# Key loads moved to the SP queue and spread over the batch, GpSimd work reordered behind the split of u, and a new deal of the value matmuls in groups that lend a PSUM bank

## The chip, the core and the metric

The kernel runs on one core of a Trainium2 chip. The metric is the device time of one execution in microseconds (us). The core has five engines with a queue of instructions each, worked off in order: TensorE (PE in the profile; its weight loads are PEld), VectorE (DVE), ScalarE (ACT), GpSimd (POOL) and SyncE (SP). SP only issues DMAs here; ACT issues some too. All DMAs are carried by the same 16 DMA engines.

## What is computed

An attention over pooled keys, then a feed-forward layer with a SoLU activation and a layer norm:

```python
kv_pool = kv.reshape(B, H // 4, 4, W // 4, 4, C).mean(axis=(2, 4))
k = v = kv_pool.reshape(B, -1, C) @ w_sr            # 4 batches, 768 keys of 128
s = (q @ k.transpose(0, 2, 1)) / sqrt(C)            # 12288 queries a batch
x = softmax(s) @ v
h = x @ w_in                                        # 128 -> 1024
solu = h * softmax(h)
ln = (solu - mean) / sqrt(var + 1e-6) * g_ln
out = ln @ w_out                                    # 1024 -> 128
```

Inputs are float32 and float64; the kernel works with float16 high and low halves, so most products are three matmuls (high by high, high by low, low by high).

## The kernel before

The queries are cut into 384 tiles of 128 (`NT`), 96 to a batch (`TPB`), four tiles to a group (`GT`). The main loop runs over slots. In one slot every stage of the pipeline does its step for another tile: the scores of tile slot+1 (`scores_pe`), their softmax and its float16 split (`scores_exp`, `scores_split`, which ends in a DMA transpose `pT` on SP), a quarter of the value matmuls of a group (`values`, 18 matmuls of 512 columns to a group), the hidden layer of tile slot-9 (`hidden_pe`), its maximum, exponential, product u, variance (`hidden_max`, `hidden_exp`, `hidden_u`, `hidden_var`) and u's float16 split on POOL (`hidden_split`, two instructions, followed by the DMA transpose `uT` on SP in `hidden_turn`), and the output layer of tile slot-13 (`final_pe`, 24 matmuls of 128 columns). From slot 9 on the order of the instructions on each engine is the order in which the code is written (`tc.manual_schedule`). I name slots by their remainder: 4n+1 is a slot with one more than a multiple of 4.

Once in four slots, on POOL: `q_low` (the low half of the next queries, slot 4n+2), the two small instructions of `final_scale` (tiles `f`, slot 4n+3) after an ACT instruction that they wait for, and `values_norm` (tiles `zz`, slot 4n+1). In slot 4n+1 DVE also does `values_split` (`xl`), `values_recip` (`rz`) and `final_out` (`ob`). On SP, a load of queries (`qf`, 256 KB) stands ahead of the pT of slot 4n+3, a store of results after the uT of slot 4n+1.

While a batch is worked on, the keys and values of the next are prepared by a table, `PLAN`: rows of slot in the batch, half (384 keys each) and functions. Each of 16 summands of the pooling is loaded in two halves of 192 KB by `kv_load` on the ACT queue, one half every second slot from slot 4 to slot 64, and added by `kv_add` on POOL three slots later. When a half has its sum, `kv_k_pe` multiplies it by w_sr, and a chain of small steps on ACT, POOL and DVE follows; half 0 does this from slot 41, half 1 from slot 69. The matmuls of this chain (`kv_k_pe`, `kv_norm_pe`, `kv_v_pe`, the slots in `WITH_PE`: 41, 69, 77, 81, 85, 89) borrow the one PSUM bank in which `values` accumulates (`ps_x`, one buffer), so a group whose values would start in such a slot deals its 18 matmuls 0, 6, 6, 6 over four slots instead of 4, 5, 5, 4. This deal is used in all four batches, though the last one prepares no keys.

PSUM also sets the rhythm of PE: scores and hidden tiles share three buffers (`ps_r`), so `scores_pe` of a slot waits until DVE has done `hidden_u`, and `hidden_pe` until DVE has done `scores_split`.

Of the kernel before, what the change touches and what calls it, by code (L numbers as in the profile page):

```python
# [11 lines left out]
F32 = mybir.dt.float32  # L12
# [27 lines left out]
LAV = 2  # L40
# [4 lines left out]
FSC = 12  # L45
# [7 lines left out]
def kernel(  # L53
# [68 lines left out]
    state = {}  # L122
# [18 lines left out]
    def half_of(name, b, half):  # L141
        return state[name, b][:, half * 384 : half * 384 + 384]
# [31 lines left out]
        )  # L174
        nc.scalar.copy(half_of("kT", 0, half), pk)

    def kv_load(b, part):

        half, pos = divmod(part, RR)
        if pos % 2 == 0:  # L180
            state["kv", b, half, pos // 2] = dmt.tile(
                [P, 2, 384], F32, tag="kvc", name=f"kv_{b}_{part}", bufs=9
            )
        r, two = divmod(pos, 2)
        k0 = two * NK + half * 384
        nc.scalar.dma_start(
            state["kv", b, half, r][:, two, :], kv[b - 1, r, :, k0 : k0 + 384]
        )

    def kv_add(b, part):  # L190

        half, pos = divmod(part, RR)
        t = state["kv", b, half, pos // 2]
        if pos == 1:
            if half == 0:
                state["ka", b] = bat.tile([P, NK], F32, tag="ka", name=f"ka_{b}", bufs=1)
            state["ka", b, half] = half_of("ka", b, half)
            x = state["kv", b, half, 0][:, 0, :]
        else:
            x = state["ka", b, half]  # L200
        nc.gpsimd.tensor_tensor(state["ka", b, half], x, t[:, pos % 2, :], op=ALU.add)

    def kv_psum(b, name):
        pool, tag = (ps_x, "x") if b else (ps_o, "o")
# [119 lines left out]
    def kv_plan(b):  # L324


        plan = {}
        for slot, half, *fs in PLAN:
            plan.setdefault(slot, []).append([partial(f, b, half) for f in fs])
        return plan  # L330


    QL = 1
# [18 lines left out]
    def q_low(g):  # L352
        if g >= NG:
            return
        qf = state["qf", g // QL][:, (g % QL) * 512 : (g % QL + 1) * 512]
        qh, ql = state["q", g]
        nc.gpsimd.tensor_tensor(ql, qf, qh.bitcast(F32), op=ALU.subtract)
# [45 lines left out]
        )  # L403


    def values(g, qtr, part):
        share = {0: [0, 0, 18, 0], 1: [0, 6, 6, 6]}.get(g, [4, 5, 5, 4])
        first = GT * g + GT - 1 + LAV
        if g > 1 and {first % TPB, first % TPB + TPB} & WITH_PE:
            share = [0, 6, 6, 6]  # L410
        s0 = sum(share[:qtr])
        s1 = s0 + share[qtr]
        if s0 == s1:
            return
        cut = s0 + (s0 > 0)
        s0, s1 = ((s0, cut), (cut, s1))[part]
        b = g * GT // TPB
        if s0 == 0 and s1:
            state["xa", g] = ps_x.tile([P, 512], F32, tag="x", name=f"xa_{g}")
        if s0 == s1:  # L420
            return
        xa, pT = state["xa", g], state["pT", g]
        vh, vl = state["vh", b], state["vl", b]
        seq = [(a, c, v) for c in range(NKC) for (a, v) in ((0, vh), (1, vh), (0, vl))]
        for n in range(s0, s1):
            a, c, v = seq[n]
# [149 lines left out]
    def final_scale(g):  # L576

        b = g * GT // TPB
        f = grp.tile([P, GT], F32, tag="f", name=f"f_{g}")
        f2 = grp.tile([P, GT], F32, tag="f2", name=f"f2_{g}")  # L580
        bb = state["bb", b]
        nc.scalar.activation(
            f2, state.pop(("z2", g)), AF.Square, scale=bb[:, 1:2], bias=bb[:, 2:3]
        )
        nc.gpsimd.tensor_tensor(f, f2, state.pop(("v3", g)), op=ALU.add)  # L585
        nc.gpsimd.tensor_tensor(f2, f, mhalf[:, :GT], op=ALU.pow)  # L586
        state["f", g] = f2

    def final_out(g):
        po, f = state.pop(("po", g)), state.pop(("f", g))  # L590
        ob = dmt.tile([P, GT, P], F32, tag="ob", name=f"ob_{g}")
        nc.vector.scalar_tensor_tensor(  # L592
            ob,
            po.rearrange("p (j c) -> p j c", j=GT),
            swi,
            f.unsqueeze(2).to_broadcast([P, GT, P]),
            op0=ALU.mult,
            op1=ALU.mult,
        )
        nc.sync.dma_start(  # L600
            out[g * 512 : (g + 1) * 512, :].rearrange("(j p) c -> p j c", p=P), ob
        )
# [121 lines left out]
    def kv_norms(half):  # L724
# [17 lines left out]

    PLAN = [(4 + 2 * r - 2 * (r // RR), r, kv_load) for r in range(2 * RR)]
    PLAN += [(7 + 2 * r - 2 * (r // RR), r, kv_add) for r in range(2 * RR) if r % RR]
    PLAN += [
        (41, 0, kv_k_pe, kv_k_out), (69, 1, kv_k_pe, kv_k_out),
        (45, 0, kv_ks), (71, 1, kv_ks),
        (48, 0, kv_kh), (72, 1, kv_kh),  # L750
        (52, 0, kv_kl), (74, 1, kv_kl),
        (56, 0, kv_sq), (75, 1, kv_sq),
        (77, 0, kv_scale_v), (78, 1, kv_scale_v), (79, 2, kv_scale_v),
        (79, 0, kv_vs), (81, 1, kv_vs),
        (77, 0, kv_norm_pe, kv_norm_out), (80, 0, kv_norm_max),
        (81, 1, kv_norm_pe, kv_norm_out), (84, 1, kv_norm_max),
        (85, 0, kv_v_pe, kv_norm_out), (87, 0, kv_v_high), (88, 0, kv_v_low),
# [2 lines left out]
    ]  # L760
    WITH_PE = {slot for slot, _, *fs in PLAN if len(fs) > 1}


    def at(t, fn, *args):
        if 0 <= t < NT:
            fn(t, *args)

    def at_last(t, fn, *args):

        if 0 <= t < NT and t % GT == GT - 1:  # L770
            fn(t // GT, *args)

    FRONT = (kv_norm_max, kv_scale_v, kv_bound)
    plan = {}
    by_hand = ExitStack()
    scores_pe(0)
    for slot in range(NT + LO + 2):
# [4 lines left out]
        i = slot - LH  # L782
        av, qtr = divmod(slot - LAV - GT + 1, GT)
        tb, ti = divmod(slot, TPB)
        if ti == 4 and tb + 1 < B:
            for k, v in kv_plan(tb + 1).items():
                plan.setdefault(slot + k - 4, []).extend(v)
        if ti == 12 and tb + 1 < B:
            kv_alloc(tb + 1)
        qs = GT if slot < 3 * GT else 3 * GT + QSP  # L790
# [7 lines left out]
        if 0 <= av < NG:  # L798
            values(av, qtr, 0)
        at(slot + 1, scores_pe)  # L800
        at_last(slot - NORM, values_norm)
        at_last(slot - FSC, final_scale)
        if slot < NT and 0 < qs < slot and (slot - 1 - qs) % GT == 0:
            q_low(slot // GT + 1)
        at(i - 1, hidden_split)
        at(i - 1, hidden_var)
        at(i, hidden_max)
        at(i, hidden_exp)
# [2 lines left out]
        for st in todo:  # L811
            if len(st) > 1:
                st[0]()
        if 0 <= av < NG:
            values(av, qtr, 1)
        for st in todo:
            for f in st[1:]:
# [3 lines left out]
        at_last(slot - NORM, values_recip_u)  # L821
        at(i + 1, hidden_pe)
        at(slot - LO, final_pe)
        at(i - 1, hidden_turn)
        at_last(slot - LO - 1, final_out)
        at_last(slot - XSP, values_out)
# [41 lines left out]
```

## Time and profile before

| what | value |
|---|---|
| median of 3 runs | 1917.81 us (1906.03 to 1918.63) |
| the profiled execution, its own time | 1920.48 us |
| its span (first to last instruction) | 1918.7 us |
| mean granted TensorE clock | 0.993 |
| PE, DVE, ACT, POOL busy | 97%, 93%, 92%, 85% |
| DMA, mean over the span | 226 GB/s |

Busy shares are unions of the instructions' spans on an engine; matmuls are pipelined, so consecutive ones overlap in the records, and a PE that is shown busy throughout streams without a hole. A row of the trace gives the start in us from the span's begin, the duration, the engine, the line in the kernel, and in square brackets the idle time of the engine ahead of it with what ended it. "SPq" is an instruction of SP's queue. Stretches below are named by their window in us.

### The profile page before, as it was taken

To read this page: it belongs to the slowest core of one execution; us is meant where nothing else is said; L and a number is where in the kernel's file an instruction comes from. 1 tells how busy PE (TensorE), PEld (TensorE's weight loads), DVE (VectorE), ACT (ScalarE), POOL (GpSimd) and SP (SyncE) were. 2 spreads that over 40 slices of the span, in tenths; PEclk is the share of its full clock that TensorE was granted. 3 is DMA by queue.
4 is the path that set the end of the run, shared out by engine and by line. 5 is a ranking of instruction groups with operands and counts; after the bars stand their busy time and mean duration, and the time that the engine had idled before them with its cause. 6 is when DMAs were issued, how large, how long until landed. Compare 5 with 4: busy or idle time off the path is not lost. (4 is left out here: it accounts for less than half of the span.)

```text
span 1918.7 us, 43085 instructions
## 1 busy us (share of the span) xinstructions
PE 1855.9 (97%) x15678; PEld 1306.6 (68%) x15678; DVE 1793.5 (93%) x2700; ACT 1760.2 (92%) x3143; POOL 1624.6 (85%) x1392
## 2 busy tenths in 40 slices
PE   7899999999999999999999999999999999999997
PEld 4576666766777666767776666666777776777665
DVE  7999989999999998999999999989999999999985
ACT  4899989999999998999999999989999999999986
POOL 4699989888899998988889989978888888888776
PEclk8999999999999999999999999999999999999999
DMA  6999999999999999999999999999999999999996
GB/s 233 178 244 238 243 228 237 234 221 216 234 240 249 236 229 233 233 237 213 223 229 239 240 229 248 232 223 214 214 225 226 218 230 228 222 223 225 222 200 139
DMA packets 1484308, 432.86 MB, mean 226 GB/s; under 512 B 1405888, under 2 KB 1471552, under 8 KB 1483840
## 3 DMA queue, kind: packets, MB, share of 16 engines
q1 hardware_dynamic: 1469840, 410.10, 108.0%
q10 hardware_dynamic: 14256, 20.00, 4.2%
q8 instruction: 124, 2.03, 0.5%
q14 instruction: 88, 0.72, 0.1%
HBM read 52.50 MB, written 25.17 MB: 40 GB/s over the span
## 5 line engine op out<-in xcount | busy, mean ns | idle before, releaser
L536 POOL TENSOR_TENSOR uhl<-u,uhl 128x1024 f16<-128x1024 f32 x384 | 819.2, 2133 | 38.5 <-ACT uhl L533 7.0
L568 PEld LDWEIGHTS <-uT 128*128 128x128 f16 x9216 | 547.5, 98 | 112.2 <-DMA uT<-uhl 28.4
L568 PE MATMUL o<-wch,uT 128*128 128x128 f16 x6144 | 580.3, 220 | 15.7 <-DMA uT<-uhl 15.7
L568 PE MATMUL o<-wcl,uT 128*128 128x128 f16 x3072 | 537.0, 220 | 0.0
L518 DVE SCALAR_TENSOR_TENSOR u<-h,rz,e 128x1024 f32<-128x1024 f32 x384 | 491.0, 1279 | 30.0 <-ACT e L504 12.6
L488 DVE TENSOR_SCALAR_CACHE_REDUCE junkd<-h,rz 128x1024 bf16<-128x1024 f32 x384 | 491.3, 1279 | 14.5 <-PE h L480 13.2
L504 ACT ACTIVATE e<-h,nm,rz 128x1024 f32<-128x1024 f32 x384 | 458.4, 1194 | 8.0 <-DVE junkd L488 8.0
L549 ACT ACTIVATE junk<-u,su 128x1024 bf16<-128x1024 f32 x384 | 437.7, 1140 | 2.8 <-DVE u L518 2.8
L535 POOL TENSOR_SCALAR uhl<-u 128x1024 f16<-128x1024 f32 x378 | 394.7, 1044 | 29.1 <-DVE u L518 19.3
L387 DVE TENSOR_REDUCE nm<-s 128x1 f32<-128x768 f32 x384 | 365.3, 951 | 50.1 <-PE s L371 44.5
L427 PE MATMUL xa<-pT,vh 128*128 128x512 f16 x1152 | 377.0, 382 | 14.1 <-issue 3.6
L388 ACT ACTIVATE s<-s,nm 128x768 f32<-128x768 f32 x384 | 335.2, 873 | 56.2 <-DVE nm L387 55.3
L398 DVE SCALAR_TENSOR_TENSOR phl<-s,phl 128x768 f16<-128x768 f32 x384 | 366.0, 953 | 5.8 <-ACT phl L390 5.8
L390 ACT ACTIVATE phl<-s 128x768 f16<-128x768 f32 x384 | 311.0, 810 | 12.0
L480 PEld LDWEIGHTS <-xh 128*128 128x128 f16 x1536 | 143.8, 98 | 200.0 <-issue 22.4
L371 PE MATMUL s<-kh,qh 128*128 128x384 f32 x768 | 256.0, 414 | 8.4 <-DVE u L518 3.9
L480 PE MATMUL h<-w_in_h,xh 128*128 128x512 f16 x768 | 229.6, 381 | 10.6 <-DVE rz L462 5.8
L480 PE MATMUL h<-w_in_h,xl 128*128 128x512 f16 x768 | 230.3, 382 | 0.0
L480 PE MATMUL h<-w_in_l,xh 128*128 128x512 f16 x768 | 230.0, 381 | 0.0
L427 PE MATMUL xa<-pT,vl 128*128 128x512 f16 x576 | 219.4, 381 | 0.0
L371 PE MATMUL s<-kh,ql 128*128 128x384 f32 x768 | 197.8, 339 | 0.0
L371 PE MATMUL s<-kl,qh 128*128 128x384 f32 x768 | 195.7, 336 | 0.0
(130 smaller groups left out, 1845.9 us busy)
## 6 DMA issues: line engine op xcount, KB each, us to landing
qf<-in_q_dram SPq DMA_DIRECT2D x96, 256.0 KB, 3.4
out_dram<-ob SPq DMA_DIRECT2D x96, 256.0 KB, 2.9
kv<-in_kv_dram ACTq DMA_DIRECT2D x96, 192.0 KB, 4.0
kv<-in_kv_dram SPq DMA_DIRECT2D x16, 384.0 KB, 8.1
pT<-phl SPq DMA_TRANSPOSE x384, 4.1
uT<-uhl SPq DMA_TRANSPOSE x384, 4.5
raw_in<-in_moe_w_in_dram ACTq DMA_DIRECT2D x1, 1024.0 KB, 6.4
raw_out<-in_moe_w_out_dram SPq DMA_DIRECT2D x1, 1024.0 KB, 7.6
```

The source lines that it names most:

```text
L371: nc.tensor.matmul(s[:, half, :384], lh[:, ts], rh[:, half * 384 : (half + 1) * 384], start=n == 0, stop=n == 2,)
L387: nc.vector.tensor_reduce(nm, s, axis=AX.XY, op=ALU.max, negate=True)
L398: nc.vector.scalar_tensor_tensor(phl[:, 1], state.pop(("s", t)), SC, phl[:, 0], op0=ALU.mult, op1=ALU.subtract)
L427: nc.tensor.matmul(xa, v[:, c, :], pT[:, :, a * NKC + c, :], start=n == 0, stop=n == len(seq) - 1)
L480: nc.tensor.matmul(h[:, hs], lh[:, ts], rh[:, hs], start=n == 0, stop=n == 2)
L488: nc.vector.tensor_scalar(junk, state["h", t], state["rz", g][1][:, j : j + 1], None, op0=ALU.mult, op1=ALU.min, accum_out=nm,)
L504: nc.scalar.activation(e, state["h", t], AF.Exp, bias=nm, scale=state["rz", g][0][:, js], accum_out=state["z2", g][:, js],)
L518: nc.vector.scalar_tensor_tensor(u, state.pop(("h", t)), state["rz", g][2][:, j : j + 1], state.pop(("e", t)), op0=ALU.mult, op1=ALU.mult, ...
L535: nc.gpsimd.tensor_scalar(uhl[:, 0, :], u, 1.0, 1.0, op0=ALU.mult, op1=ALU.mult)
L536: nc.gpsimd.tensor_tensor(uhl[:, 1, :], u, uhl[:, 0, :], op=ALU.subtract)
L549: nc.scalar.activation(junk, u, AF.Square, scale=-float(DFF), bias=su, accum_out=state["v3", g][:, j : j + 1],)
L568: nc.tensor.matmul(po[:, ts], uT[:, a * NFC + c, :], w[:, c, :], start=c == 0 and n == 0, stop=c == NFC - 1 and n == 2,)
```

## The change

1. **Loads.** `kv_load` now loads both halves of a summand at once (384 KB, rows of 3072 B instead of 1536 B) and is issued by SP, at the end of its slot. For batch 1 one load comes every 4 slots from slot 4 to slot 64; for batches 2 and 3 one every 6 slots, from 30 slots before the preceding batch begins (slot 66 of the batch before that) to slot 60 of the preceding batch.
2. **Adds.** The 30 adds of a batch stay, on POOL; the first half's comes 4 slots after its load, the second's 6 slots after. All stand in even slots now; they stood in odd ones.
3. **Key chain.** Both halves go through the chain in slots 69 to 92; half 0 no longer starts in slot 41, half 1 starts its product in slot 73. So the groups that lend their bank are those of slots 69, 73, 77, 81, 85, 89.
4. **Deal of values.** Such a group deals 3, 5, 5, 5, and the first 3 stand at the slot's end, behind `final_pe`. Only batches that prepare keys for another do this; the last batch keeps 4, 5, 5, 4.
5. **POOL order.** The two POOL instructions of `final_scale` become `final_root`, and these and `q_low` are called after `hidden_split`; they stood before it.

```diff
-    def kv_load(b, part):
-        half, pos = divmod(part, RR)
...
-        nc.scalar.dma_start(
-            state["kv", b, half, r][:, two, :], kv[b - 1, r, :, k0 : k0 + 384]
-        )
+    def kv_load(b, pos):
+        t = dmt.tile([P, 2, 384], F32, tag="kvc", name=f"kv_{b}_{pos}", bufs=9)
         r, two = divmod(pos, 2)
+        nc.sync.dma_start(
+            t, kv[b - 1, r, :, two * NK : (two + 1) * NK].rearrange("p (h k) -> p h k", h=2)
+        )
...
+        first, step = (4, 4) if b == 1 else (-30, 6)
+        for pos in range(RR):
+            slot = first + step * pos
+            yield slot, [partial(kv_load, b, pos)]
+            if pos:
+                yield slot + 4, [partial(kv_add, b, 0, pos)]
+                yield slot + 6, [partial(kv_add, b, 1, pos)]
         for slot, half, *fs in PLAN:
+            yield slot, [partial(f, b, half) for f in fs]
...
+    def with_keys(g):
+        b, ti = divmod(GT * g + GT - 1 + LAV, TPB)
+        return g > 1 and b + 1 < B and ti in WITH_PE
...
-        first = GT * g + GT - 1 + LAV
-        if g > 1 and {first % TPB, first % TPB + TPB} & WITH_PE:
-            share = [0, 6, 6, 6]
+        if with_keys(g):
+            share = [3, 5, 5, 5]
...
-        (41, 0, kv_k_pe, kv_k_out), (69, 1, kv_k_pe, kv_k_out),
+        (69, 0, kv_k_pe, kv_k_out), (73, 1, kv_k_pe, kv_k_out),
...
+        at(i - 1, hidden_split)
+        at_last(slot - FSC, final_root)
         if slot < NT and 0 < qs < slot and (slot - 1 - qs) % GT == 0:
             q_low(slot // GT + 1)
-        at(i - 1, hidden_split)
...
-        if 0 <= av < NG:
+        late = 0 <= av < NG and qtr == 0 and with_keys(av)
+        if 0 <= av < NG and not late:
             values(av, qtr, 1)
...
         at(slot - LO, final_pe)
+        if late:
+            values(av, qtr, 1)
```

SP after the change, in the early part of batch 0; `kv` are the loads that stood on ACT's queue, the other names are the transposes, the store (`out`) and the queries (`qf`):

```order
L397 DMA_TRANSPOSE pT_1801<-phl_1775 128x12x128
L542 DMA_TRANSPOSE uT_1835<-uhl_1788 128x16x128
L181 DMA kv_6_1841<-in_kv_dram 128x768
L397 DMA_TRANSPOSE pT_1801<-phl_1846 128x12x128
L542 DMA_TRANSPOSE uT_1916<-uhl_1863 128x16x128
L604 DMA out_dram<-ob_1918 128x4x128
L397 DMA_TRANSPOSE pT_1801<-phl_1927 128x12x128
L542 DMA_TRANSPOSE uT_1988<-uhl_1940 128x16x128
L336 DMA qf_2000<-in_q_dram 128x512
```

A load now stands in the same queue between one slot's uT and the next slot's pT; there was nothing between these two before, and the loads stood on ACT between two exponentials.

POOL over four slots of batch 0, before:

```order
L585 TENSOR_TENSOR f_2605<-f_6_2606,v_6_2183 128x4
L586 TENSOR_TENSOR f_6_2606<-f_2605,mhalf 128x4
L535 TENSOR_SCALAR uhl_2610<-u_2592 128x1024
L536 TENSOR_TENSOR uhl_2610<-u_2592,uhl_2610 128x1024
L201 TENSOR_TENSOR ka_536<-kv_16_2292 128x384
```

and after:

```order
L536 TENSOR_SCALAR uhl_2596<-u_2580 128x1024
L537 TENSOR_TENSOR uhl_2596<-u_2580,uhl_2596 128x1024
L590 TENSOR_TENSOR f_2593<-f_6_2594,v_6_2175 128x4
L591 TENSOR_TENSOR f_6_2594<-f_2593,mhalf 128x4
L536 TENSOR_SCALAR uhl_2664<-u_2653 128x1024
```

The two `f` instructions moved from ahead of a slot's `uhl` pair to behind it; `ql` moved in the same way.

PE in slot 77, the first norm matmul of the key chain (`pn`), after the change, up to the next slot's scores (`s`); `xa` are the values:

```order
L231 MATMUL pn_0_5388<-ksq_619,ones_87 128x384
...
L569 MATMUL o_5404<-wch,uT_5281 128x128
L428 LDWEIGHTS vh_113
L428 MATMUL xa_5429<-pT_5017,vh_113 128x512
...
L428 MATMUL xa_5429<-pT_5017,vl_114 128x512
L428 LDWEIGHTS vh_113
L428 MATMUL xa_5429<-pT_5017,vh_113 128x512
L367 MATMUL s_5453<-kh_105,qh_5140 128x384 x2
```

Four matmuls of values (three of this slot, one of the next) now stand between the output layer's last matmul and the next scores; before, the scores followed the output layer directly.

## Rows read from the trace of the kernel before

**Rows 1.** The page: its head, and part 2's data rate in 40 slices.
```profile
span 1918.7 us, 43085 instructions
GB/s 233 178 244 238 243 228 237 234 221 216 234 240 249 236 229 233 233 237 213 223 229 239 240 229 248 232 223 214 214 225 226 218 230 228 222 223 225 222 200 139
```

**Rows 2.** Windows: from:to, length, busy PE PEld DVE ACT POOL, PEclk, DMA, GB/s.
```profile
1420.00:1600.00 180.00, 180.00 (x1569) 128.14 (x1568) 175.41 (x260) 172.74 (x310) 150.00 (x125) 1.00 1.13 227
712.00:722.00 10.00, 8.04 (x66) 5.37 (x64) 7.68 (x14) 8.06 (x16) 9.56 (x9) 0.83 1.25 239
1255.00:1270.00 15.00, 11.75 (x80) 7.70 (x79) 9.42 (x15) 9.09 (x17) 10.21 (x9) 0.77 1.23 201
```

**Rows 3.** Tile xh, one instruction a group: count, min/median/max ns, first to last start.
```profile
L434 ACT ACTIVATE xh<-xa,sv x9: 687/687/687, 1434.0 to 1583.5; 128x512 f16<-128x512 f32 x9
L434 ACT ACTIVATE xh<-xa,sv x13: 687/687/687, 114.9 to 347.7; 128x512 f16<-128x512 f32 x13
L434 ACT ACTIVATE xh<-xa,sv x11: 687/687/687, 614.4 to 810.3; 128x512 f16<-128x512 f32 x11
L434 ACT ACTIVATE xh<-xa,sv x13: 687/687/687, 1039.8 to 1279.4; 128x512 f16<-128x512 f32 x13
L434 ACT ACTIVATE xh<-xa,sv x7: 687/687/687, 347.7 to 464.9; 128x512 f16<-128x512 f32 x7
L434 ACT ACTIVATE xh<-xa,sv x23: 687/687/687, 1434.0 to 1850.0; 128x512 f16<-128x512 f32 x23
```

**Rows 4.** Waits: engine and line, releaser: us in total, times, longest.
```profile
PEld L568 <- DMA uT<-uhl: 28.4, 33, 3.3
PE o L568 <- DMA uT<-uhl: 15.7, 17, 3.2
```

**Rows 5.** Tile uT: issue to landing, first in 1420:1740, then in 100:350.
```profile
DMA to landing us min/median/max: 3.7/4.0/6.3
DMA to landing us min/median/max: 3.8/4.9/7.6
```

**Rows 6.** Timeline of DVE and SP in 243:262.
```profile
246.38 0.95 DVE L398 SCALAR_TENSOR_TENSOR phl<-s,phl 128x768 f16<-128x768 f32 x1
254.75 1.42 SPq L401 DMA_TRANSPOSE pT<-phl  x1
```

**Rows 7.** Tile pT, SP's issues in 150:317.4 and in 336:372.
```profile
L401 SPq DMA_TRANSPOSE pT<-phl x35: 1279/1465/4191, 150.1 to 317.4; - x35
L401 SPq DMA_TRANSPOSE pT<-phl x9: 1279/1433/1782, 336.6 to 371.5; - x9
```

**Rows 8.** The page, part 6: issues, KB each, median us to landing.
```profile
kv<-in_kv_dram ACTq DMA_DIRECT2D x96, 192.0 KB, 4.0
kv<-in_kv_dram SPq DMA_DIRECT2D x16, 384.0 KB, 8.1
```

**Rows 9.** Waits of POOL for ACT.
```profile
POOL f L585 <- ACT f L582: 129.9, 92, 6.2
POOL ql L357 <- ACT qh L349: 34.0, 39, 8.3
```

**Rows 10.** Timeline of POOL and PE in batch 3, slots 4n+2 and 4n+3.
```profile
1627.42 1.27 POOL L357 TENSOR_TENSOR ql<-qf,qh 128x512 fp32r<-128x512 f32 x1 [1.07 <-ACT qh L349]
1628.67 1.05 POOL L535 TENSOR_SCALAR uhl<-u 128x1024 f16<-128x1024 f32 x1
1629.80 2.13 POOL L536 TENSOR_TENSOR uhl<-u,uhl 128x1024 f16<-128x1024 f32 x1
1634.64 0.51 PE L371 MATMUL s<-kh,ql 128*128 128x384 f32 x2
```

**Rows 11.** Timeline of PE and ACT in batch 0, slots 85 (429 to 432) and 78 (393).
```profile
393.39 0.62 PE L371 MATMUL s<-kh,qh 128*128 128x384 f32 x2 [0.15 <-DVE u L518]
...
429.62 0.59 PE L480 MATMUL h<-w_in_h,xh 128*128 128x512 f16 x2 [0.29 <-DVE rz L462]
429.93 0.47 ACT L245 COPY vf<-pv 128x384 f32<-128x384 f32 x1
432.19 0.22 PE L568 MATMUL o<-wch,uT 128*128 128x128 f16 x1
```

More of the change, by code (lines that the diff above doesn't have):

```diff
@@ L175, in kv_first_k, with kv_add @@
         nc.scalar.copy(half_of("kT", 0, half), pk)
-    def kv_load(b, part):
-        half, pos = divmod(part, RR)
-        if pos % 2 == 0:
-            state["kv", b, half, pos // 2] = dmt.tile(
-                [P, 2, 384], F32, tag="kvc", name=f"kv_{b}_{part}", bufs=9
-            )
+    def kv_load(b, pos):
+        t = dmt.tile([P, 2, 384], F32, tag="kvc", name=f"kv_{b}_{pos}", bufs=9)
         r, two = divmod(pos, 2)
-        k0 = two * NK + half * 384
-        nc.scalar.dma_start(
-            state["kv", b, half, r][:, two, :], kv[b - 1, r, :, k0 : k0 + 384]
-        )
[L190 to L201, printed above, removed]
+        nc.sync.dma_start(
+            t, kv[b - 1, r, :, two * NK : (two + 1) * NK].rearrange("p (h k) -> p h k", h=2)
+        )
+        state["kv", b, pos] = t
+    def kv_add(b, half, pos):
+        if pos == 1 and half == 0:
+            state["ka", b] = bat.tile([P, NK], F32, tag="ka", name=f"ka_{b}", bufs=1)
+        ka = half_of("ka", b, half)
+        x = state["kv", b, 0][:, half, :] if pos == 1 else ka
+        nc.gpsimd.tensor_tensor(ka, x, state["kv", b, pos][:, half, :], op=ALU.add)
     def kv_psum(b, name):
@@ L324, in kv_plan @@
     def kv_plan(b):
-        plan = {}
+        first, step = (4, 4) if b == 1 else (-30, 6)
[5 more added lines that the diff above has]
+                yield slot + 6, [partial(kv_add, b, 1, pos)]
         for slot, half, *fs in PLAN:
-            plan.setdefault(slot, []).append([partial(f, b, half) for f in fs])
-        return plan
+            yield slot, [partial(f, b, half) for f in fs]
     QL = 1
@@ L584, in final_scale, with final_root @@
         )
+        state["f", g] = (f, f2)
+    def final_root(g):
+        f, f2 = state["f", g]
         nc.gpsimd.tensor_tensor(f, f2, state.pop(("v3", g)), op=ALU.add)
         nc.gpsimd.tensor_tensor(f2, f, mhalf[:, :GT], op=ALU.pow)
-        state["f", g] = f2
     def final_out(g):
-        po, f = state.pop(("po", g)), state.pop(("f", g))
+        po, (_, f) = state.pop(("po", g)), state.pop(("f", g))
         ob = dmt.tile([P, GT, P], F32, tag="ob", name=f"ob_{g}")
@@ L741 @@
     }
-    PLAN = [(4 + 2 * r - 2 * (r // RR), r, kv_load) for r in range(2 * RR)]
-    PLAN += [(7 + 2 * r - 2 * (r // RR), r, kv_add) for r in range(2 * RR) if r % RR]
-    PLAN += [
-        (41, 0, kv_k_pe, kv_k_out), (69, 1, kv_k_pe, kv_k_out),
[L749 to L754, printed above, removed]
+    PLAN = [
+        (69, 0, kv_k_pe, kv_k_out), (73, 1, kv_k_pe, kv_k_out),
+        (71, 0, kv_ks), (74, 1, kv_ks),
+        (72, 0, kv_kh), (75, 1, kv_kh),
+        (73, 0, kv_kl), (76, 1, kv_kl),
+        (74, 0, kv_sq), (76, 1, kv_sq),
+        (78, 0, kv_scale_v), (79, 1, kv_scale_v), (80, 2, kv_scale_v),
+        (80, 0, kv_vs), (82, 1, kv_vs),
         (77, 0, kv_norm_pe, kv_norm_out), (80, 0, kv_norm_max),
@@ L774 @@
     plan = {}
+    for b in range(1, B):
+        for k, fs in kv_plan(b):
+            plan.setdefault((b - 1) * TPB + k, []).append(fs)
     by_hand = ExitStack()
@@ L784 @@
         tb, ti = divmod(slot, TPB)
-        if ti == 4 and tb + 1 < B:
-            for k, v in kv_plan(tb + 1).items():
-                plan.setdefault(slot + k - 4, []).extend(v)
         if ti == 12 and tb + 1 < B:
```

## The prediction

> **What bounds the kernel now.** I read the page first, then windows of the trace, then one instruction that occurs once a group, then the waits and SP's queue.
>
> The span is 1918.7 us [rows 1]. In a quiet window of batch 3, in which no keys are prepared, PE is busy in 180.00 of 180 us [rows 2]. So PE streams there without a hole, and no other engine could make those groups shorter. The first row of xh, ACT's one instruction a group, tells how long a group then takes: nine of them lie between 1434.0 and 1583.5, eight intervals, 149.5/8 = 18.69 us a group, 4.67 us a slot [rows 3]. This is the floor, and the question is only where groups take longer. I go through the other rows of xh [rows 3] and subtract 18.69 a group:
>
> - While key loads run: batch 0, 12 groups, 232.8 us, 8.5 too long; batch 1, 10 groups, 195.9 us, 9.0 too long; batch 2, 12 groups, 239.6 us, 15.3 too long. Together 32.8 us.
> - While the key chain runs (slots 69 to 92): 6 groups in 117.2 us, 5.1 too long. The two like stretches of batches 1 and 2 (from 810.3 and from 1279.4) take the same 117.2. Together 15.2 us.
> - Batch 3: 22 groups in 416.0 us, 4.8 too long. Nothing is loaded or prepared there; six of these groups still deal 0, 6, 6, 6, so this is the price of the deal alone, 0.8 a group.
>
> So some 53 us of the span are not streaming. A group with the old deal in slot 41 sits in each load stretch, at about 1.0; the rest of the 32.8 are holes in irregular places.
>
> **Whose holes these are.** PE and its weight loads wait for the transposed u (uT) 17 and 33 times [rows 4], and not because the transposes are long by themselves: a uT lands after a median of 4.0 us in the quiet window and of 4.9 us, at worst 7.6, while loads run [rows 5]. The delay piles up in SP's queue. At 247.33 (246.38 + 0.95) DVE has finished a phl; SP issues its transpose at 254.75, 7.4 us later [rows 6]. From 150.1 to 317.4 SP issues 35 of them, 34 intervals, 4.92 us each; from 336.6 to 371.5, just after the last load, 8 intervals at 4.36 us while it catches up [rows 7]. I take 4.36 as what the DMA engines need for a slot without key loads, and 4.92 with them. Against PE's 4.67 this is a surplus of 0.31 and a deficit of 0.25. The difference, 0.56 a slot, is one 192 KB load every second slot: 1.12 us of the queue's time each.
>
> Over the 60 slots of the loads the deficit makes 15.0 us of lag in batch 0. PE lost 8.5 less the 1.0 of slot 41, 7.5; so some 7.5 us were absorbed by the head start that the transposes have in quiet times. Where the lag reached PE with a hole of some us, the clock followed: granted 0.83 in 712 to 722 and 0.77 in 1255 to 1270, where PE also stands idle for 2 and 3.3 us [rows 2]; these are stretches at the lower level of 1.2 GHz instead of 2.4, and they cost 1.7 and 3.4 us (10 x 0.17, 15 x 0.23) that belong to the 32.8.
>
> **The change, part by part.** *Loads on SP.* The bytes are the same. How long 384 KB hold the queue on SP in the midst of transposes, no row shows. Bounds: the best slice moved 249 GB/s [rows 1], 393216 B at that rate are 1.58 us; at the page's mean of 226 GB/s, 1.74 us; and two of the loads on ACT's queue cost 2 x 1.12 = 2.24 us. The loads on SP at the start land after 8.1 us against 4.0 on ACT [rows 8], but sixteen of those are queued behind each other, so this is a wait in line. I take 1.58 to 1.74: one queue that is worked off in order has no second stream to share the engines with, and the rate is one that this mix of transfers reached. Batch 0 then needs 4.36 + 1.58/4 = 4.76 to 4.80 us a slot, a deficit of 0.09 to 0.13, over 60 slots 5 to 8 us of lag, about what was absorbed without loss (7.5). In batches 1 and 2, with a load every 6 slots, 4.36 + 1.58/6 = 4.62 to 4.65, just under PE's 4.67: no new lag, but little to work off an old one. With single late transposes I leave 2 us a batch: 32.8 becomes 6, a gain of 26.8, the holes at the lower clock included. At 2.24 it would be 18 (first rival). ACT loses 96 issues and SP takes 48; SP's own issuing fits, since a transpose of pT takes 1.4 us there [rows 7].
>
> The Trainium skill, page "DMA: Bandwidth & Descriptors", section "Issuing engines are not separate DMA queues", says that transfers issued by several engines run on the same 16 engines and interleave, and that another issuing engine saves only the sequencer's time. By it the move to SP alone gains nothing, and only the wider spread counts; this is the first rival below.
>
> *POOL's order.* POOL waits 129.9 us for ACT's part of f, 92 times, 1.4 us each, and 34.0 us for qh, both ahead of the split of u [rows 9]. Behind the split these waits and the instructions themselves no longer delay uhl, in one slot of four by 1.4 us and the two f's, in another by ql. In quiet stretches nobody waits for that (PE has no hole), so its price is nothing there; it adds head start to the uT of the slots concerned, which is why I do not go above 2 us a batch. What is late instead is ql. In the quiet rows ql ends at 1628.69 and PE uses it at 1634.64 [rows 10]; the split takes 3.26 us (1628.67 to 1631.93), after it ql ends at about 1633.2, so 1.4 us are left. Cost nothing, as long as POOL begins that split on time; it idled 1.07 us just before [rows 10]. The adds, same number, keep their place behind all this in even slots.
>
> *The key chain.* In slot 4n+1 PE comes to the hidden layer early, since values are missing ahead of it, and waits for DVE (0.29 us after the transposes of v) [rows 11]. The new deal leaves that wait: values still stand behind. It removes a second one, the scores' wait for u in the next slot (0.15) [rows 11], since four value matmuls now stand in between. They need the bank, that is ACT's copy: it ends at 430.40 while the output layer's last matmul starts at 432.19, 1.8 us of cover [rows 11]; were that gone, each us would be paid 18 times. Before, five of the six groups lent their bank, now six, and both halves' steps lie in slots 69 to 76, some 1.7 us more of ACT there, where ACT idles 7.26 us in 180, 0.75 a group [rows 2]. I take 15.2 to 14.6, bounds 10 and 20. A first product in slot 69 of batch 0 follows its add in slot 68 closely; at most one add's length, 1 us, once.
>
> *Batch 3* has no keys to prepare and goes back to 4, 5, 5, 4: 4.8 to 0, the surest term.
>
> **The sum.** 26.8 + 0.6 + 4.8 = 32.2. The profiled execution took 1920.48 us, 1.8 above its span and 2.7 above the median; 1920.5 - 32.2 = 1888.3, say **1888 us**. The groups of 18.69 remain, and so do start and end.
>
> **Rivals.** *The load costs the same on SP.* A load of 384 KB holds the queue 2.24 us. Batch 0 stays at 4.92 a slot and loses its 7.5; batches 1 and 2 need 4.36 + 2.24/6 = 4.73, 0.06 over, 90 slots, 5.4 each: 18.3 instead of 6, 1900 us. For it: same bytes, same engines. Against it: a slot moves 1.048 MB (its two transposes by their shapes, 128x1536 and 128x2048 of two bytes, and a quarter of the 512 KB of qf and out), 240 GB/s at 4.36; with 98 KB of keys it is 1.147 MB, only 233 GB/s at 4.92, so the mixing of two queues seems to cost something.
>
> *The lag is never worked off.* Before, six groups without loads followed each stretch of loads, and SP caught up by 0.31 a slot [rows 7]. Now the loads for batch 2 begin in slot 66, two slots after the last of batch 1, and some stand just ahead of qf and of the group's last pT. If the 0.02 to 0.05 a slot that I leave are not there, every late transpose reaches PE in all three batches: at 0.5 us a group, 72 groups, 36 us instead of 32.8, 1918 us. For it: the surplus is thin. Against it: the long holes came at the end of 60 slots with a deficit of 0.25, which no stretch has any more.
>
> *Slower: ql comes too late.* Every group's scores need it. If POOL starts the split of slot 4n+2 later than 1.4 us after u, PE waits for the rest once a group. To end 1% above the median it must cost some 50 us, 0.7 a group in the 72 groups of three batches, so a lag of 2.1 us, every time; 1938 us. For it: an add (1.0) in slot 4n and zz in 4n+1 stand ahead. Against it: slot 4n+1 is DVE's longest, and POOL idled before ql.
>
> **Chances.** Forecast 0.68 (1877 to 1898), the same cost on SP 0.17, lag never worked off 0.09, ql too late 0.06. A measurement of this kernel can tell about 1% from no change, 19 us, so faster means below 1898.6: 0.68 and a small part of the second case, 0.70. Within 1%: 0.24. Slower: 0.06. The range reaches down to no loss under loads and 10 in the chain (1877) and up past the second case to 1905; outside lie the third and fourth cases and a little on the low side.
>
> **What would show it.** Intervals of xh of about 18.8 in the load stretches and 18.69 throughout batch 3; SP issuing pT close behind phl, at most some 5 us late at the end of batch 0's loads; no stretch of the lower clock between 100 and 1850 us; POOL's wait for f gone from ahead of the split. Wrong is the load's price if SP falls behind in batches 1 and 2, the POOL step if PE waits for ql before the third pair of scores, and the chain if value matmuls wait for ACT's copy.

## The result, and the profile after

The changed kernel takes 1894.38 us (median of 4 runs, 1893.94 to 1894.88). The kernel before, run beside it, took 1915.05 (4 runs); over the 31 runs of it that e5 to e8 below share, its median is 1910.9 (1905 to 1921). The ratio is 0.9909, 95% interval 0.9884 to 0.9935: faster, by a little under 1%. The profiled execution of before, 1920.48 us, was one of its slowest, so the difference of the two profiles, 25.6 us (1920.48 - 1894.88), is about 9 us more than the difference of the medians, 16.5 (1910.9 - 1894.4).

All profile rows below are in the forms of the groups shown above. The page of the kernel after, its head, against [rows 1]:

```profile
span 1893.1 us, 43052 instructions
```

Windows of the kernel after, against [rows 2]: the quiet window of batch 3, and everything from the first slots to the last.

```profile
1420.00:1600.00 180.00, 180.00 (x1553) 127.59 (x1552) 175.25 (x260) 173.04 (x309) 151.88 (x127) 1.00 1.15 223
45.00:1874.00 1829.00, 1800.90 (x15464) 1274.34 (x15463) 1762.75 (x2654) 1735.04 (x3104) 1593.35 (x1365) 1.00 1.16 229
```

The granted clock is 1.00 throughout; the two stretches at 0.83 and 0.77 of before have no counterpart between the first slots and the last. PE is idle for 28.1 us of 1829.

Tile xh after, one instruction a group, against [rows 3]: loads and key stretch of batches 0, 1 and 2, then batch 3.

```profile
L435 ACT ACTIVATE xh<-xa,sv x13: 687/687/687, 115.3 to 343.7; 128x512 f16<-128x512 f32 x13
L435 ACT ACTIVATE xh<-xa,sv x7: 680/687/687, 343.7 to 463.8; 128x512 f16<-128x512 f32 x7
L435 ACT ACTIVATE xh<-xa,sv x11: 687/687/687, 613.3 to 800.4; 128x512 f16<-128x512 f32 x11
L435 ACT ACTIVATE xh<-xa,sv x7: 679/687/687, 800.4 to 919.0; 128x512 f16<-128x512 f32 x7
L435 ACT ACTIVATE xh<-xa,sv x13: 687/687/687, 1031.7 to 1257.0; 128x512 f16<-128x512 f32 x13
L435 ACT ACTIVATE xh<-xa,sv x7: 677/687/687, 1257.0 to 1374.7; 128x512 f16<-128x512 f32 x7
L435 ACT ACTIVATE xh<-xa,sv x23: 687/687/687, 1412.1 to 1823.3; 128x512 f16<-128x512 f32 x23
```

With the same floor of 18.69 us a group, the first row is 12 groups in 228.4 us, 4.1 too long, and so on (starts are shown to 0.1 us, so a sum over three batches is good to some 0.2):

| us above the floor | before | forecast | after |
|---|---|---|---|
| load stretches, batches 0, 1, 2 | 8.5 + 9.0 + 15.3 = 32.8 | 6 | 4.1 + 0.2 + 1.0 = 5.3 |
| key stretches | 5.06 x 3 = 15.2 | 14.6 | 8.0 + 6.5 + 5.6 = 20.1 |
| batch 3 | 4.8 | 0 | 0.0 |

The profile gave 27.5 under loads and 4.8 in batch 3, and lost 4.9 in the key stretches and some 1.8 elsewhere (1.1 behind the last of these groups, 0.4 in the start): 25.6 in all. The loads are what changed most; the key stretch went the wrong way.

Waits after (us in total, times, longest), against [rows 4] and [rows 9]:

```profile
PEld L569 <- DMA uT<-uhl: 14.7, 16, 3.3
PE o L569 <- DMA uT<-uhl: 8.9, 9, 3.0
POOL uhl L536 <- DVE u L519: 153.6, 128, 7.6
POOL ql L353 <- ACT qh L345: 11.3, 2, 8.6
```

PE's waits for transposes are about half of before's 28.4 and 15.7. POOL's wait for ACT's part of f is gone, and of its 39 waits for qh two remain; nearly all of its waiting is now for u.

Landing of uT after, in 100:350, against the second line of [rows 5], and SP's pT in slots 27 to 61 of batch 0, against [rows 7]:

```profile
DMA to landing us min/median/max: 3.8/4.6/7.1
L397 SPq DMA_TRANSPOSE pT<-phl x35: 1273/1451/2615, 150.8 to 313.5; - x35
```

34 intervals in 162.7 us are 4.785 us a slot, where before had 4.92 and the forecast said 4.76 to 4.80. In slots 4 to 66 the latest pT of each batch is issued 5.0, 3.1 and 4.9 us after DVE has finished its phl; before it was 7.4, 6.4 and 7.5.

**Where the key stretch lost.** Two instructions of 128x1 elements on DVE got up to ten times as long. They add and maximise two columns of the key chain's scale (`sv`, slot 78, one slot earlier before the change) and bound (`knm`, slot 88). One of the four stands in the kernel's start; it is short before and after. First the kernel before, then after (count, min/median/max ns):

```profile
L255 DVE TENSOR_TENSOR sv<-kss x4: 148/149/149, 34.2 to 1316.7; 128x1 f32<-128x1 f32 x4
L272 DVE TENSOR_TENSOR knm<-knm x4: 149/150/151, 53.2 to 1370.3; 128x1 f32<-128x1 f32 x4
```

```profile
L246 DVE TENSOR_TENSOR sv<-kss x4: 149/1041/1515, 35.1 to 1300.8; 128x1 f32<-128x1 f32 x4
L263 DVE TENSOR_TENSOR knm<-knm x4: 151/1486/1492, 53.4 to 1348.1; 128x1 f32<-128x1 f32 x4
```

The timeline of the kernel after shows what they stand against, in slots 77 and 78 and in 88 and 89 of batch 1 (start, duration, engine; in brackets the idle time ahead and what ended it):

```profile
843.57 2.13 POOL L537 TENSOR_TENSOR uhl<-u,uhl 128x1024 f16<-128x1024 f32 x1
843.72 0.59 PE L481 MATMUL h<-w_in_h,xh 128*128 128x512 f16 x2 [0.59 <-DVE rz L463]
844.21 1.51 DVE L246 TENSOR_TENSOR sv<-kss 128x1 f32<-128x1 f32 x1
847.84 0.62 PE L367 MATMUL s<-kh,qh 128*128 128x384 f32 x2 [0.46 <-DVE u L519]
...
891.80 2.14 POOL L537 TENSOR_TENSOR uhl<-u,uhl 128x1024 f16<-128x1024 f32 x1
892.46 1.49 DVE L263 TENSOR_TENSOR knm<-knm 128x1 f32<-128x1 f32 x1
903.85 0.59 PE L481 MATMUL h<-w_in_h,xh 128*128 128x512 f16 x2 [1.03 <-DVE rz L463]
```

Both end with POOL's subtraction: 844.21 + 1.51 = 845.72 beside 843.57 + 2.13 = 845.70, and 892.46 + 1.49 = 893.95 beside 893.94. DVE stands for 1.35 us each time, and PE, 2 and 10 us after that, for 0.46 and 1.03. The Trainium skill, page "SBUF — State Buffer", section "Who interferes with whom", says just this: a DVE instruction with two operands in SBUF and a GpSimd instruction that reads SBUF lock each other out, and the later one stands until the other ends. The trace agrees for the subtraction (1.51 us against 0.149): in all the profiles together, each of the 34 of these additions and maxima that began inside it ended with it, within 0.02 us. The kernel before, in batch 1:

```profile
847.62 0.15 DVE L255 TENSOR_TENSOR sv<-kss 128x1 f32<-128x1 f32 x1
847.63 2.13 POOL L536 TENSOR_TENSOR uhl<-u,uhl 128x1024 f16<-128x1024 f32 x1
...
900.36 1.02 POOL L586 TENSOR_TENSOR f<-f,mhalf 128x4 f32<-128x4 f32 x1
901.22 0.15 DVE L272 TENSOR_TENSOR knm<-knm 128x1 f32<-128x1 f32 x1
```

There `sv` began 0.01 us ahead of the subtraction, and `knm` stood beside POOL's power of 128x4. Neither was held: 0.15 us both times, so not every GpSimd instruction that reads SBUF costs the DVE one its whole length.

### The profile page after: what moved, and what is told of

Its sections match the earlier page's. It is cut to its first block, busy times and chain, and to the rows that moved or that the text cites. A ratio compares the mean times of both kernels' runs of the same rounds, so it can differ in the third digit from the quotient of the medians.

```text
span 1893.1 us, 43052 instructions
## 1 busy us (share of the span) xinstructions
PE 1843.6 (97%) x15677; PEld 1303.5 (69%) x15678; DVE 1797.0 (95%) x2700; ACT 1758.1 (93%) x3143; POOL 1621.6 (86%) x1392
## 3 DMA queue, kind: packets, MB, share of 16 engines
q10 hardware_dynamic: 432, 1.12, 0.2%
## 5 line engine op out<-in xcount | busy, mean ns | idle before, releaser
L481 PE MATMUL h<-w_in_h,xh 128*128 128x512 f16 x768 | 228.4, 379 | 12.0 <-DVE rz L463 7.1
L481 PE MATMUL h<-w_in_h,xl 128*128 128x512 f16 x768 | 228.4, 379 | 0.0
```

What stands on the lines that cost most here:

```text
L481: nc.tensor.matmul(h[:, hs], lh[:, ts], rh[:, hs], start=n == 0, stop=n == 2)
```

## Experiments

Times are medians; the ratio is that to the kernel before, with its 95% interval. "Loads" and "keys" are the sums over three batches above 18.69 us a group, from the first and last xh of the same stretches as in the table above. The expectations count keys by the output layer's first matmul of a group, which gives 1.2 to 1.4 us less for the same sum (after 18.7, e4 14.5, e9 13.9) and puts as much more under loads (after 6.6): a late transpose on the border of the two stretches falls to the one or the other. One profile each: the loads of batch 0 alone lie between 4.1 and 8.9 us in the kernels that load as the changed one does.

| kernel | us | ratio | loads | keys | batch 3 |
|---|---|---|---|---|---|
| after | 1894.4 | 0.9909 [0.9884, 0.9935] | 5.3 | 20.1 | 0.0 |
| e1_act_queue | 1901.5 | 0.9939 [0.9916, 0.9961] | 15.5 | 18.5 | 0.1 |
| e2_pool_before | 1893.1 | 0.9914 [0.9881, 0.9947] | 6.3 | 16.8 | 0.0 |
| e3_every_4 | 1904.0 | 0.9967 [0.9950, 0.9985] | 15.0 | 19.2 | 0.1 |
| e4_one_input | 1890.7 | 0.9900 [0.9870, 0.9929] | 9.3 | 15.7 | 0.1 |
| e5_deal_0666 | 1900.8 | 0.9934 [0.9916, 0.9952] | 10.2 | 24.6 | 0.0 |
| e6_before_sp | 1905.9 | 0.9973 [0.9954, 0.9991] | 23.8 | 15.6 | 4.9 |
| e7_before_pool | 1916.0 | 1.0029 [1.0013, 1.0046] | 22.5 | 18.5 | 4.9 |
| e8_final_first | 1903.0 | 0.9958 [0.9941, 0.9975] | 10.3 | 26.0 | 0.0 |
| e9_deal_3456 | 1890.2 | 0.9891 [0.9869, 0.9913] | 7.2 | 15.1 | 0.0 |
| e10_mixed | 1888.5 | 0.9880 [0.9854, 0.9906] | 4.8 | 13.8 | 0.0 |
| e11_halves | 1897.4 | 0.9926 [0.9899, 0.9953] | 8.0 | 21.5 | 0.0 |

**The loads: queue, spread or size?** e1 is the changed kernel with the loads back on ACT's queue:

```diff
-        nc.sync.dma_start(
+        nc.scalar.dma_start(
             t, kv[b - 1, r, :, two * NK : ...
```

> The changed kernel with its 48 loads of 384 KB issued by ACT again instead of SP; sizes, slots, deal and POOL order as changed. If one queue is what made a load cheap (theory): a load holds the transposes up for about 2.2 us again, batch 0's loads cost PE some 7 us and those of batches 1 and 2 about 5 each, 18 instead of the 6.7 measured in the load stretches; some 1905 us, uT and pT land later, and SP is several us behind in batches 1 and 2. If size and spread alone did it (rival): 1894 within 2 us.

Its ten runs lie in two clusters, 1894 to 1897 and 1901 to 1906. In batch 0, where the loads are densest, it loses less than the changed kernel:

```profile
L435 ACT ACTIVATE xh<-xa,sv x13: 687/687/687, 114.6 to 340.2; 128x512 f16<-128x512 f32 x13
L397 SPq DMA_TRANSPOSE pT<-phl x35: 1279/1442/3213, 148.3 to 308.3; - x35
```

225.6 us for 12 groups, 1.3 too long against 4.1; SP goes at 4.706 us a slot. So ACT's queue isn't dearer per load, and the median is 7 us longer all the same; in the profile batches 1 and 2 lose 5.0 and 9.2, most of it in two single holes. (The changed kernel ran four times, 1893.9 to 1894.9; that it has no second cluster is not shown by so few.) The timeline of the largest, and its window:

```profile
1164.45 2.53 SPq L542 DMA_TRANSPOSE uT<-uhl  x1
1165.31 0.33 ACTq L181 DMA_DIRECT2D kv<-in_kv_dram  x1
1174.36 0.29 PE L569 MATMUL o<-wch,uT 128*128 128x128 f16 x1 [3.19 <-DMA uT<-uhl]
```

```profile
1165.00:1180.00 15.00, 11.81 (x81) 8.55 (x79) 9.91 (x16) 9.59 (x18) 10.74 (x9) 0.78 1.24 185
```

A uT issued at 1164.45 lands 9.9 us later, the load issued 0.9 us behind it on the other queue takes 8.8; the data rate falls to 185 GB/s, and PE stands idle for 3.2 us; part of the window runs at the lower level of 1.2 GHz, 0.78 in its mean, as in the two holes of before. Such a hole with a clock dip stands in the load stretches of before (two), e1 (two) and e7 (one), which load on ACT throughout; of the nine kernels that load on SP throughout, only e3 has one (0.83 in 212 to 222), which is enough to say that two queues are not needed for it. What the DMA engines do in such a hole isn't shown.

e6 is the kernel before with its 192 KB loads on SP, and nothing else:

```diff
-        nc.scalar.dma_start(
+        nc.sync.dma_start(
             state["kv", b, half, r][:, two, :], ...
```

> The kernel before with its loads of 192 KB issued by SP in the same slots; nothing else. If one queue makes a load cheaper (theory): 4.36 + 0.4 = 4.76 to 4.80 us a slot instead of 4.92, the load stretches lose some 3 to 6 us a batch instead of 7.5 to 14, about 1900 us. If the queue does not matter (rival): within 4 us of the kernel before, 1915.

```profile
L401 SPq DMA_TRANSPOSE pT<-phl x35: 1285/1502/3041, 151.2 to 319.1; - x35
```

167.9 us, 4.938 a slot, where before had 4.92: a load of 192 KB on SP holds the transposes as long as one on ACT, 1.16 us against 1.12. The queue alone gives 0.3% (0.9973), 5.0 us between the medians, so the time lies between theory and rival. Where these 5 us come from is not shown: the profile, of a run of 1911.8, has no hole with a lower clock but loses 23.8 under loads. The Trainium skill's rule that I had set against the move ("DMA: Bandwidth & Descriptors", section "Issuing engines are not separate DMA queues", that another issuing engine saves only the sequencer's time) agrees with the mean price of 192 KB. For 384 KB ACT is the cheaper queue, 1.38 at most against the 1.70 to 2.14 worked out below. Issuing a load takes 0.57 us of SP's own queue, which is of the size of that difference:

```profile
L181 SPq DMA_DIRECT2D kv<-in_kv_dram x14: 567/572/1832, 99.9 to 342.5; - x14
```

But e6's loads take SP the same 0.57 and show no such difference, so this isn't shown as its cause.

e3 takes the spread away: all three batches load every 4 slots.

```diff
-        first, step = (4, 4) if b == 1 else (-30, 6)
+        first, step = (4, 4)
```

> The changed kernel with the loads of batches 2 and 3 in slots 4 to 64, one every 4, as batch 1's are. If the wider spread matters (theory, 4.76 us a slot against 4.67): batches 1 and 2 lose about as much under loads as batch 0 does (5.2 us each, against 0.1 and 1.4 measured), 9 us more, some 1903 us; a part comes back in the key stretch, which then has no adds beside it (0.8 us in the group of slot 77, twice). If the queue alone did it (rival): 1894 within 2 us.

Batches 1 and 2 lose 5.0 and 3.0 us where the changed kernel loses 0.2 and 1.0, and the time is 9.6 us longer, of a gain of 16.5: as the theory said, the spread carries most of it. In the profiles 6.8 of the 9.7 us more under loads lie in batches 1 and 2; the rest lies in batch 0, whose loads are the same in both kernels, so it says only how far single profiles differ. The edit moves the adds on POOL along with the loads, and the two were not tried apart.

e11 asks whether the larger piece is cheaper: each load as two of 192 KB on SP, one behind the other.

```diff
-        nc.sync.dma_start(
-            t, kv[b - 1, r, :, two * NK : (two + 1) * NK].rearrange(...)
-        )
+        for h in range(2):
+            k0 = two * NK + h * 384
+            nc.sync.dma_start(t[:, h, :], kv[b - 1, r, :, k0 : k0 + 384])
```

> The changed kernel with each 384 KB load issued by SP as two of 192 KB, one right after the other. Theory, that the larger piece makes a load cheaper: a pair holds the transposes for 2 x 1.16 = 2.3 us instead of 1.7, which is above the 1.87 us that six slots of PE's pace win back; SP's pace in batch 0 goes from 4.78 to about 4.94 us a slot, the load stretches lose 7 to 8 us more in batch 0 and 5 to 7 us more in each of batches 1 and 2, 1908 to 1914 us. Rival, that only the spread and the one queue count and not the size: pace and stretches as in the changed kernel, 1893 to 1896 us.

```profile
L397 SPq DMA_TRANSPOSE pT<-phl x35: 1279/1521/3451, 148.8 to 315.9; - x35
```

167.1/34 = 4.915 a slot, so (4.915 - 4.36) x 4 = 2.22 us for the pair. By the same working 384 KB in one piece on SP come to 1.70 in the changed kernel, 1.85 in e2, and 2.02 to 2.14 in e3, e4, e5, e8 and e9. Starting one slot later the pair comes to 2.18 and e5 to 2.28, so the pair is not told apart from the upper of these. The 14 to 20 us that the theory of the size expected did not come: 1897.4, 3 us more than the changed kernel, with overlapping intervals, and batches 1 and 2 lost no more (0.0 and 1.2). Nearer to the rival, outside its 1893 to 1896.

**POOL's order and the tiny instructions.** e2 is the changed kernel with the calls of `final_root` and `q_low` ahead of `hidden_split` again; e7 is the kernel before with POOL's new order.

```diff
-        at(i - 1, hidden_split)
         at_last(slot - FSC, final_root)
         if slot < NT and 0 < qs < slot and (slot - 1 - qs) % GT == 0:
             q_low(slot // GT + 1)
+        at(i - 1, hidden_split)
```

> The changed kernel with POOL's old order: f's two instructions and ql ahead of the split of u. If the loads made the gain (theory): the load stretches stay within 3 us of the 6.7 measured, 1892 to 1897 us. If the earlier split made it (rival): the holes return, 10 to 20 us more in the load stretches, above 1904 us. Second point: in the key stretch DVE's 128x1 additions and maxima of two inputs, which took 1.5 us beside POOL's split, should then be short again (0.15 us) if POOL's timing made them long, and the key stretch 2 to 3 us shorter.

> The kernel before with POOL's new order alone: f's two instructions and ql behind the split of u. If the loads made the gain (theory): at most 5 us faster, 1910 to 1915, and SP still 4 to 7 us behind under loads. If the earlier split made it (rival): the uT holes go, 1900 or less.

e2's `knm` and e7's `knm`:

```profile
L263 DVE TENSOR_TENSOR knm<-knm x4: 147/149/151, 53.0 to 1345.9; 128x1 f32<-128x1 f32 x4
```

```profile
L272 DVE TENSOR_TENSOR knm<-knm x4: 147/1536/1545, 52.7 to 1362.3; 128x1 f32<-128x1 f32 x4
```

For `knm` the order decides whether it runs into POOL's subtraction: 1.5 us with the new one in both kernels, 0.15 with the old. For `sv` it doesn't decide alone. First e7, then e2:

```profile
L255 DVE TENSOR_TENSOR sv<-kss x4: 149/151/152, 34.3 to 1308.7; 128x1 f32<-128x1 f32 x4
L246 DVE TENSOR_TENSOR sv<-kss x4: 150/151/1352, 33.7 to 1297.8; 128x1 f32<-128x1 f32 x4
```

With the new order and the old key chain it is never held, with the old order and the new chain once in three batches: its new place in slot 78 has a part in it. The keys cost 18.5 instead of 15.2 in e7 and 16.8 instead of 20.1 in e2; e7 is slower than before by 0.29% (1.3 to 4.6 in a thousand), 5.1 us between the medians. The order alone thus lost time, 3.3 us of it in the key stretch of the profile. And it didn't make the gain, as the theories said: e2 keeps its short loads (6.3) and its time (1893.1), and e7 still loses 22.5 under loads.

e4 leaves the order and takes the second operand away:

```diff
-            nc.vector.tensor_tensor(sv[:, 0:1], kss[:, 0:1], kss[:, 1:2], op=ALU.add)
+            nc.vector.tensor_reduce(sv[:, 0:1], kss, axis=AX.X, op=ALU.add)
...
-            nc.vector.tensor_tensor(knm[:, 0:1], knm[:, 0:1], knm[:, 1:2], op=ALU.max)
+            nc.vector.tensor_reduce(knm[:, 0:1], knm, axis=AX.X, op=ALU.max)
```

> The changed kernel with the two DVE instructions that read two operands in SBUF in the key chain (the sum of kss and the maximum of knm, 128x1 each) written as reductions over two columns, which read one. If these wait for POOL's split (theory): they take 0.2 us instead of 0.9 and 1.2 us on average, the groups of slots 77 and 89 lose 0.7 to 1.0 us less each, 3 to 4 us in all, 1890 to 1891 us. If DVE is late there for another reason, such as waiting for ACT's sums (rival): they stay long or the next instruction becomes so, 1894 within 1 us.

```profile
845.66 2.13 POOL L537 TENSOR_TENSOR uhl<-u,uhl 128x1024 f16<-128x1024 f32 x1
846.28 0.15 DVE L246 TENSOR_REDUCE sv<-kss 128x1 f32<-128x2 f32 x1
846.35 0.95 DVE L383 TENSOR_REDUCE nm<-s 128x1 f32<-128x768 f32 x1
```

In the same place, 0.6 us into the same subtraction, the instruction takes 0.15 us. The wait of PE for u in slot 78 and the one of 1.03 us in slot 89 are gone, the keys cost 15.7 instead of 20.1, and the time is 1890.7, as expected. Of the 5.5 us that the key stretches took beyond the forecast, this is 4.4.

**The deal.** e5 is the changed kernel with the old deal:

```diff
-            share = [3, 5, 5, 5]
+            share = [0, 6, 6, 6]
```

> The changed kernel with the deal 0, 6, 6, 6 in the groups that lend their bank (only in batches that prepare keys). If the new deal gives and takes about the same (theory: the wait for u in the next slot goes, the wait for DVE's split of the softmax grows by one matmul, 0.2 us): within 2 us of 1894. If the new deal is what made the key stretch longer than before (18.1 us against 15.2; rival): 3 us shorter, 1891.

PE's waits of over 0.4 us in slots 77, 78, 89 and 90 of batch 1, to be set beside 0.59, 0.46 and 1.03 above:

```profile
849.88 0.59 PE L481 MATMUL h<-w_in_h,xh 128*128 128x512 f16 x2 [0.54 <-DVE rz L463]
854.02 0.62 PE L367 MATMUL s<-kh,qh 128*128 128x384 f32 x2 [1.34 <-DVE u L519]
...
910.62 0.59 PE L481 MATMUL h<-w_in_h,xh 128*128 128x512 f16 x2 [0.81 <-DVE rz L463]
913.94 0.62 PE L367 MATMUL s<-kh,qh 128*128 128x384 f32 x2 [0.52 <-DVE u L519]
```

The wait for u that the values cover stands open again, at 1.34 us where DVE was held: 24.6 us for the keys, 6.4 us more time, where theory and rival had both put it at no more than 2. The 0.52 of slot 90 needs no held DVE; the kernel before has it too:

```profile
914.89 0.62 PE L371 MATMUL s<-kh,qh 128*128 128x384 f32 x2 [0.53 <-DVE u L518]
```

e8 (with e4's reductions) puts the output layer ahead of the hidden layer in the slots that lend a bank, to cover the wait for rz:

```diff
+        if late:
+            at(slot - LO, final_pe)
         at(i + 1, hidden_pe)
-        at(slot - LO, final_pe)
         if late:
             values(av, qtr, 1)
+        else:
+            at(slot - LO, final_pe)
```

> The changed kernel with the two reductions of one input, and in slots that lend the bank PE's output layer (24 matmuls, 1.37 us) ahead of its hidden layer instead of behind it. If PE's wait ahead of the hidden layer is what is left in the key stretch (theory): the wait of 0.4 to 1.0 us is filled with these matmuls, the groups lose little more than the key matmuls themselves (0.4 to 0.85 us a group), 12 us or less instead of 18, about 1887 us. If DVE then gets its hidden tile too late (rival): the wait comes back one slot later, 1890 or more.

```profile
831.71 0.22 PE L569 MATMUL o<-wch,uT 128*128 128x128 f16 x1 [0.45 <-DVE ob L596]
871.61 0.22 PE L569 MATMUL o<-wch,uT 128*128 128x128 f16 x1 [0.92 <-DVE ob L596]
```

The output layer now waits for `ob`, which empties the bank it writes (0.45 us in slot 73, 0.92 in slot 81), a wait that neither theory nor rival had. What follows is late, as the rival said: in batch 1 DVE waits 0.76 us for the hidden tile of slot 77. The keys cost 26.0 us, and the time is 12 us longer than e4's; the order of the changed kernel is the better one.

e9 (with e4's reductions) deals one block less ahead:

```diff
-            share = [3, 5, 5, 5]
+            share = [3, 4, 5, 6]
```

> The changed kernel with the two tiny two-input additions as one-input reductions (which alone gave 1890.7 us) and the lent groups' values dealt 3, 4, 5, 6 from the slot's end instead of 3, 5, 5, 5. Theory, that a lent bank's release at the chain's start decides what is left of the key stretch: one block fewer lies in front of the bank copies in the second and third slot, so the key stretch falls from 14.5 to about 12.5 us over its three batches and the time to about 1888.5 us. Rival, that the deal was already past the point where it binds: key stretch 14 to 15 us, 1890 to 1891.5 us.

```profile
844.37 0.59 PE L481 MATMUL h<-w_in_h,xh 128*128 128x512 f16 x2 [0.59 <-DVE rz L463]
863.63 0.59 PE L481 MATMUL h<-w_in_h,xh 128*128 128x512 f16 x2 [0.22 <-DVE rz L463]
```

With 3, 5, 5, 5 and the reductions, in e4, the same two waits for rz in slots 77 and 81 are 0.60 and 0.29. e9's keys cost 15.1, its time is 1890.2. The rival holds: from 3, 5, 5, 5 on the deal no longer binds. What makes rz late in slot 77 was not tried.

e10 is e9 with ACT's queue for batch 1's keys alone, the 16 loads that come densely in batch 0 (not eight, as the expectation says):

```diff
+        queue = nc.scalar if b == 1 else nc.sync
-        nc.sync.dma_start(
+        queue.dma_start(
```

> The kernel before this one in the list, with the eight loads of batch 1's keys (the ones every 4 slots in batch 0) issued by ACT and the later ones by SP. Theory, that ACT's queue is no dearer on average and takes the loads out of the row that the transposes stand in: batch 0 loses 1 to 2 us instead of 5 to 10, batches 1 and 2 as before, about 1884 us. Rival, that ACT's queue brings rare long landings wherever the loads lie: batch 0 has a single group that loses 3 us or more, and the time stays at 1888 us or goes above it.

```profile
L436 ACT ACTIVATE xh<-xa,sv x13: 687/687/688, 115.3 to 340.7; 128x512 f16<-128x512 f32 x13
L398 SPq DMA_TRANSPOSE pT<-phl x35: 1279/1433/2777, 149.5 to 308.9; - x35
```

Batch 0 loses 1.1 us, against 6.9 in e9, and SP goes at 4.69 a slot, PE's own pace. So its price is that of the theory, but the time that of the rival, without the rival's cause: batch 0 has no group that loses 3 us. Of these 5.8 us 1.8 arrive in the median (1888.5; six runs from 1883.2 to 1891.9); in the profile batch 2 lost 2.6 instead of 0.2. The intervals overlap, so e9 and e10 are not told apart. Both are faster in the median than the changed kernel; e10's interval and the changed kernel's overlap.

## Why the prediction came out as it did

The time, 1894.4, lies in the range, 6 us above the forecast of 1888. In the profiled run, 6.6 above it, 5.5 are the key stretches and 1.8 lie elsewhere, less 0.7 under loads. The bound for "faster by over 1%" I had put at 1898.6, from the median of three runs; in the comparison the gain is 0.9%, within the 1% to which I gave 0.24.

- **Reading the floor and the three kinds of stretches** held: 18.69 us a group is still the quiet pace, and the terms add up to the measured time.
- **Load stretches, 6 against 5.3 (profile).** The size was right, in part by luck: the five other kernels that load in the same pieces, slots and queue lose 6.3 to 10.3 in their profiles. The reason was half right. The spread does it (e3), as the step on batches 1 and 2 said. That one queue makes a load cheaper was wrong: 192 KB cost 1.16 us on SP and 1.12 on ACT (e6), and 384 KB on ACT cost at most (4.706 - 4.36) x 4 = 1.38 (e1), less than on SP. The price of 1.58 to 1.74 lay at or under the low end of the 1.70 to 2.14 that seven kernels show; that more was absorbed without loss than I had allowed for is the likely reason why the size came out, but no run shows it by itself. What SP's queue may save is the rare long hole; no run explains these. SP's 0.57 us of issuing a load I had put at nothing.
- **The sum's base.** I subtracted from 1920.48, a run with two such holes. The median of before is 10 us lower; e6 and e7, which load as densely as before, lose 23.8 and 22.5 us under loads in their profiles, not 32.8. A gain of 27 under loads is that of this profile; by these two, that of a typical run is nearer to 17. The forecast time did not suffer, since the holes stand in the base and in the gain and drop out of the difference; the gain that I announced was too large.
- **POOL's order, "Cost nothing", was wrong**, the failed step of the sum. I followed POOL's instructions to who waits for their results, and found nobody but ql. I did not ask which DVE instructions they would now run beside. Its subtraction held two tiny ones for up to 1.36 us each, `knm` by the new order, `sv` by the new order and the chain's new slots together. The old order gives back 3.3 us of the key stretches (e2), one-input instructions 4.4 (e4), and the new order made alone costs 5.1 (e7). The ql rival fell: PE never waited for ql, as the cover of 1.4 us said.
- **The key stretch, 14.6 against 20.1.** That the wait for rz remains was right, and no value matmul waited for ACT's bank copy. But the deal is worth more than the 0.6 I gave it: without it 4.5 us more in the key stretches and 6.4 in the time (e5). I had read the price of the scores' wait, 0.15, off slot 78 alone; slot 90 of the kernel before has 0.53, and with DVE held slot 78 has 1.34. What the deal is worth with DVE not held was not run. With the held instructions freed, 15.7 (e4), near the forecast.
- **Batch 3, 0,** came out exactly, and e6 and e7, which keep the old deal there, still lose 4.9.
- **"The lag is never worked off"** fell: batch 1 lost 0.2.

## What to carry to other kernels

When instructions are moved on GpSimd, list the VectorE instructions that will run beside them, and of these the ones with two operands in SBUF: even one of 128x1 elements, begun inside a long GpSimd subtraction, lasted here as long as what was left of it. Bulk loads that compete with a tight stream of transposes are best spread so thin that each one's price is won back before the next; who issues them mattered less here (5 us for the queue, 9.6 for the spread). And take the base of a sum from a typical run, or say by how much the profiled one is off before trusting the difference.

## What the chip showed that I had not expected

- A DVE addition of 128x1 with two operands in SBUF took 1.51 us beside a GpSimd subtraction of 2.13 us, a 128x2 reduction with one operand 0.15 us at the same place.
- Single DMAs on two queues at once: a transpose that usually lands after 4.8 us and a 384 KB load of 4.4 us took 9.9 and 8.8 us together, and the granted clock in the 15 us around was 0.78. Holes with a lower clock come at most twice in the loop of a profile, once with SP's queue alone (e3); the cause stays open.
- A load of 384 KB on ACT's queue delayed SP's transposes by at most 1.38 us, one on SP's own by 1.70 to 2.14.
- Beside a GpSimd power of 128x4 that took 1.02 us, the DVE maximum of 128x1 took its usual 0.15 us.
